# Cosine attention followed by mixture-of-depths: five reorderings around norms, scatters and the last batch

## The chip, the cores and the metric

The kernel runs on one core of a Trainium2 chip. The metric is the device time of one execution in microseconds. A core has five engines with queues of their own, which work in the order of their queues and wait for one another on semaphores: TensorE (PE in the profile; its weight loads are PEld), VectorE (DVE), ScalarE (ACT), GpSimd (POOL) and SyncE (SP, which here only issues transfers).

## The reference

Two parts, one after the other, on 8 batches of 448 tokens.

```python
q_n = q / (np.linalg.norm(q, axis=-1, keepdims=True) + 1e-06)      # 8 x 12 heads x 448 x 64
k_n = k / (np.linalg.norm(k, axis=-1, keepdims=True) + 1e-06)
scores = np.matmul(q_n, k_n.transpose(0, 1, 3, 2)) / tau           # tau = 0.1
attn = softmax(scores);  x = np.matmul(attn, v)                    # heads side by side: 8 x 448 x 768
scores = np.einsum('bsd,d->bs', x, w_gate)
for b in range(B):
    top_idx = np.argpartition(-scores[b], capacity)[:capacity]     # 128 of 448 tokens
    ye = np.maximum(x[b, top_idx] @ w1, 0.0) @ w2                  # 768 -> 1024 -> 768
    g = 1.0 / (1.0 + np.exp(-scores[b, top_idx]))
    out[b, top_idx] = x[b, top_idx] + g[:, None] * ye              # all other tokens: out = x
```

## The kernel before

**Slots.** The 12 heads of a batch are taken as 6 pairs, so there are 48 pairs. The main loop has one slot for each pair. All that is issued in a slot is written out in program order by hand; nothing reorders it later. In slot i the kernel computes the scores of pair i in four pieces c = 0, 3, 1, 2 (`scores`, L273 and L278) and their exponentials (`exps`, L286 and L289); multiplies the exponentials of pair i-1 with v (`pv_tails`, `pv`, L302 and L313); divides and writes pair i-1 of x (`pv_evac`, L329 and L331); transposes q and k of pair i+1 (`transposes`, L255, and its copy out of PSUM, `qkT_copy`, L261); and scales q and k of pair i+2 by their norms on GpSimd (`scale`, L228), which also casts v (`values`, L235) and the finished part of x (`half_x`, L352).

**Norms.** A pair's squares are made on ScalarE (`square`, L185) in the slot that the table `SQ` names, mostly five slots ahead. A slot later TensorE adds them up in groups of eight (`sum_pe`, L192) and VectorE finishes the sum (`sum_dve`, L200). The pairs of a group in the list `NORMS` then share three small steps: `norm_a` on ScalarE (Ln, then Exp of half, for the square root; L208 and L209), `norm_b` on GpSimd (adds 1e-6; L215) and `norm_c` on VectorE (reciprocal; L218). A group of two is done every second slot. `norm_b` stands at the end of the slot, behind `scale`, `values` and `half_x` on GpSimd; `norm_c` stands in the next slot, ahead of gate, x and the copy of the transposed tiles on VectorE. The list `due` carries a group from one to the other; where the first pair of a group is scaled in the same slot, `norm_b` and `norm_c` follow `norm_a` directly.

**Mixture of depths.** When a batch of x is done, its second part is spread over the slots after it. `work` holds functions by slot and place; the places are run in this order within a slot: P1, D0, D1, P1b, A, P2, C, D3, B. The dictionaries `late`, `mid`, `early` and `last` give the slots for each batch, counted from s = 6(b+1), the first slot after the batch.

- `gate` (L359): a product with w_gate and its sum, one column of 128 tokens at a time, on VectorE.
- `rank_prep` (L370 to L373): splits the gates in fp32 into three bf16 terms, on GpSimd.
- `rank_rep` (L391, L395, L398): TensorE spreads the terms over all partitions; with the copy `own` back to one column for each partition.
- `rank_count` (L404): for each token the number of larger gates. `pick` (L412): the 0/1 selection matrix `sel` of 128 by 128, in bf16. Both on VectorE; the last two counts and the four selections stand at place D3 of the batch's rank slot (12, 18, 24, 30, 36, 41 and 46 for batches 0 to 6).
- `select` and `select_b` (L421 to L438): row numbers and gates of the selected tokens.
- `gather` (L461), `ffn1` (L479), `ffn2` (L488): products with the selection, with w1 and with w2; the results leave PSUM by `evac` on VectorE (L443 to L447) or ScalarE (L449).
- `scatter` (L503): an indirect transfer issued by GpSimd that adds the result to the rows of the output. It runs at place P2, behind `half_x` of that slot, in the slot of the last `ffn2`.
- `store_x` (L344, L345): SyncE writes a batch of x to the output. Transfers to the output wait for the ones before it, so a store waits for an earlier scatter to land, and a scatter for the stores.

**The last batch** can't hide behind later slots. The first 640 of its 768 columns are stored early and their part of the gates is summed early (`gc`). The last 128 columns come as `x_last` behind the main loop: they are stored into a copy of the batch in memory (`x_copy`, from which the rows are gathered again as `xs`, L697) and into the output, the gates are completed and counted, and batch 6's two feed-forward layers run beside this. At the end stand the scatter of batch 6 (L503), the gather of `xs` (L697), the sum of `xs` and the result (L709) and the last scatter (L712), all scatters and the gather in GpSimd's queue.

**Loads.** q, k and v come from SyncE in groups of three pairs into a ring of four buffers. A load waits until the group that had its buffer is scaled and cast.

Of the kernel before, what the change touches and what calls it, by code (L numbers as in the profile page):

```python
# [8 lines left out]
FP32 = mybir.dt.float32  # L9
# [8 lines left out]
def kernel(  # L18
# [60 lines left out]
    starts = {g0: gi for gi, (g0, gn) in enumerate(GROUPS)}  # L79
    place = {g0 + g: (gi, g) for gi, (g0, gn) in enumerate(GROUPS) for g in range(gn)}  # L80

    NORMS = [(0, 1), (1, 2)]
    while sum(NORMS[-1]) < N:
        NORMS.append((sum(NORMS[-1]), min(2, N - sum(NORMS[-1]))))
    nplace = {g0 + g: (n, g) for n, (g0, gn) in enumerate(NORMS) for g in range(gn)}
# [76 lines left out]
    w1_sb = const.tile([P, KD, F], BF16)  # L162
    w2_sb = const.tile([P, KF, D], BF16)

    for j in range(NS):
        nc.gpsimd.affine_select(
            out=tie[:, j, :], in_=tie[:, j, :], compare_op=ALU.is_ge,
            fill=-(2.0 ** -126), base=-j * P if j < NC else T - SM, pattern=[[1, S]],
            channel_multiplier=-1)
# [44 lines left out]
    def norm_b(n):  # L214
        nc.gpsimd.tensor_scalar_add(norm_of(n), norm_of(n), 1e-6)  # L215
# [146 lines left out]
            op0=ALU.mult, op1=ALU.add, accum_out=dst[:, j:j + 1])  # L362


    def rank_prep(b, eng=None):
        g = gates[b % 2]
        eng = eng or nc.gpsimd
        sg = moe.tile([P, NS, 3], BF16, name="sg")
        r1 = moe.tile([P, NS], FP32, name="r1")
        eng.tensor_copy(sg[:, :, 0], g)  # L370
        eng.tensor_sub(r1, g, sg[:, :, 0])
        eng.tensor_copy(sg[:, :, 1], r1)
        eng.tensor_sub(sg[:, :, 2], r1, sg[:, :, 1])  # L373
        st[b]["sg"] = sg
# [10 lines left out]
    def rank_rep(b):  # L385
        sg = st[b]["sg"]
        rep = bank()
        for j in range(NS):
            c0, n = (j * P, P) if j < NC else (SM, T)
            for e in range(3):  # L390
                nc.tensor.matmul(out=rep[:, c0:c0 + n],  # L391
                                 lhsT=sg[:, j, e:e + 1].to_broadcast([P, P]),
                                 rhs=iden_b[:, P - n:], start=(e == 0), stop=(e == 2))
        for e in range(3):
            nc.tensor.matmul(out=rep[:, S:S + NS], lhsT=iden_b, rhs=sg[:, :, e],  # L395
                             start=(e == 0), stop=(e == 2))
        own = moe.tile([P, NS], FP32, name="own")
        nc.vector.tensor_copy(own, rep[:, S:S + NS])  # L398
        st[b].update(rep=rep, own=own)

    def rank_count(b, j):
        r = slice(0, P) if j < NC else slice(T, P)
# [108 lines left out]
    def at(slot, where, fn, *args):  # L511
        work.setdefault((slot, where), []).append((fn, args))

    def run(slot, where):
        for fn, args in work.pop((slot, where), []):
# [2 lines left out]

    late = dict(gate=((2, "D1"), (3, "D1"), (4, "D1"), (5, "D1")), rep=5, rank=6, select=7,
                ffn=((8, "B"), (9, "B"), (10, "B"), (11, "A")))  # L520
    mid = dict(late, ffn=((8, "B"), (9, "A"), (9, "B"), (10, "A")))
    early = dict(gate=((2, "D1"), (3, "D1"), (3, "D1"), (4, "D1")), rep=4, rank=5,
                 select=6, ffn=((7, "B"), (8, "A"), (8, "B"), (9, "A")))
    last = dict(gate=((1, "D1"), (2, "D1"), (2, "D1"), (3, "D1")), rep=3, rank=4,
                select=5, ffn=())
    for b in range(B - 1):
# [15 lines left out]
        if b < B - 2:  # L542
            at(s + m["select"] + 1, "A", gather, b, 1)
        for (d, w), (fn, n) in zip(m["ffn"], ((ffn1, 0), (ffn1, 1), (ffn2, 0), (ffn2, 1))):
            at(s + d, w, fn, b, n)
            if fn is ffn2 and n == 1:
                at(s + d, "P2", scatter, b)
    bb = B - 1
    gc = const.tile([P, NS], FP32)

# [7 lines left out]

    SQ = {}
    for p in range(3, N):  # L560
        SQ.setdefault({3: 0, 4: 0, 5: 1, 6: 2}.get(p, p - 5), []).append(p)
    SW = 2 * NB7 * D8

    wps = bank()
# [11 lines left out]
    for ps in ((0,), (1, 2)):  # L576
        sc = ps_sc.tile([P, 2, 512], FP32, name="sc")
        for p in ps:
            square(p)
        sums(ps, sc)  # L580
        for m, p in enumerate(ps):
            sum_dve(p, sc[:, 1, m * SW:(m + 1) * SW])
        norm_a(nplace[ps[0]][0])
        norm_b(nplace[ps[0]][0])
        norm_c(nplace[ps[0]][0])
        if ps[0] == 0:
            warm(24)
            scale(0, True)
            transposes(0)
            qkT_copy(0)  # L590
        else:
            scale(1)
    values(0)
    values(1)

# [1 line left out]
    for i in range(N + 1):  # L597
# [10 lines left out]
        if prev:  # L608
            pv_tails(i - 1)
        exps(i, 0)  # L610
        for p in SQ.get(i, []):
            square(p)
        run(i, "D0")
        sc = ps_sc.tile([P, 2, 512], FP32, name="sc")
# [25 lines left out]
            qkT_copy(i + 1)  # L640
        scores(i, 2)
        exps(i, 2)
        if i < 2:
            transposes(i + 1)
            qkT_copy(i + 1)
        if i + 2 < N:
            scale(i + 2)
            values(i + 2)
        if prev:
            half_x(i - 1)  # L650
        due = [n for n in due if NORMS[n][0] != i + 2]
        for n in due:
            norm_b(n)
        run(i, "P2")
        run(i, "C")
        run(i, "D3")
# [10 lines left out]
    pv(N - 1)  # L667
    pv_evac(N - 1)
    gather(b, 1, "A", True)
    store_x(bb, x_last, 5 * P, D, x_copy)  # L670
    store_x(bb, x_last, 5 * P, D)
    g7 = gates[bb % 2]
    xg = moe.tile([P, P], FP32, name="xg", bufs=1)
    nc.gpsimd.tensor_mul(xg, x_last[:, NC], wg_b[:, 5 * P:D])
    for j in range(NC):
        gate(bb, j, 5 * P, D, gc, g7, x_last)
    xgs = moe.tile([P, P], FP32, name="xgs", bufs=1)
    gd = moe.tile([P, 1], FP32, name="gd", bufs=1)
    nc.scalar.activation(xgs, xg, AF.Copy, accum_out=gd)
    nc.vector.tensor_add(g7[:, NC:], gd, gc[:, NC:])  # L680
    ffn1(b, 0, "A", True)
    rank_prep(bb, nc.vector)
    nc.scalar.activation(xh_last, x_last, AF.Copy)
    ffn1(b, 1, "A", True, 0, lambda: rank_rep(bb))
    ffn2(b, 0, "A", True)
    ffn2(b, 1, "A", True)
    for j in range(NS):
# [62 lines left out]
```

## Time and profile before

Three runs gave 280.02 us (median), from 279.03 to 280.46. The profiled execution has a span of 281.0 us.

| engine | busy us | share of the span | instructions |
|---|---|---|---|
| TensorE | 234.4 | 83% | 4591 |
| TensorE's weight loads | 176.0 | 63% | 4591 |
| VectorE | 178.5 | 64% | 477 |
| ScalarE | 203.3 | 72% | 318 |
| GpSimd | 166.9 | 59% | 228 |

The busy share is an average over slots with different limits. Slots in which ScalarE sets the pace last about 4.05 us; slots with feed-forward or selection work last 4.5 to 6 us; slot 33 lasted 8.5 us. A row of the profile's waits names the waiting instruction, the one that ended the wait, the sum of the waits in us, how often, and the longest. A timeline row has the start, the duration, the engine, the line and the operands of an instruction, or of several alike (x4); in brackets stands the idle time before it and what ended that.

### The profile page before, as it was taken

The page shows a single profiled execution, that of the slowest core. Times are in us where ns is not written, and L with a number is a line of the kernel's source. Part 1 is how long each engine was busy: PE and PEld are TensorE (multiplying, and loading weights), DVE is VectorE, ACT ScalarE, POOL GpSimd, SP SyncE. Part 2 cuts the span into 40 slices and gives each one's busy share as a digit, 9 for nine tenths or more (in the row PEclk, how much of TensorE's full clock was granted, in tenths as well). Part 3 has the DMA queues.
Part 4 walks back from the last instruction along what each step waited for, and adds up shares of the span by engine and source line. Part 5 has one row for each costly group of instructions (what it writes and reads, how often), then busy time and mean ns, then how long its engine had stood idle before and what let it go on. Part 6 is the DMA issues. An engine that isn't in the chain of part 4 may idle for free. (4 is left out here: it accounts for less than half of the span.)

```text
span 281.0 us, 10601 instructions
## 1 busy us (share of the span) xinstructions
PE 234.4 (83%) x4591; PEld 176.0 (63%) x4591; DVE 178.5 (64%) x477; ACT 203.3 (72%) x318; POOL 166.9 (59%) x228
## 2 busy tenths in 40 slices
PE   7498787688899979988979979699899798979970
PEld 6377565456677757756657757476685576657750
DVE  1333544456877786758864786467877778788611
ACT  3779999967988778869775778578776884665410
POOL 5447578849666677459471777357755864651231
PEclk9979999959999999999997999799999999986995
DMA  7999999999999849994799449992760164046851
GB/s 256 283 278 288 301 296 303 301 236 282 272 303 248 213 65 210 277 265 75 178 264 272 104 58 206 274 264 51 119 138 3 11 135 113 3 59 155 240 93 77
DMA packets 32431, 53.18 MB, mean 189 GB/s; under 512 B 2176, under 2 KB 28672, under 8 KB 31488
## 3 DMA queue, kind: packets, MB, share of 16 engines
q1 hardware_dynamic: 28976, 45.13, 60.0%
q0 software_dynamic: 2992, 6.69, 14.0%
q8 instruction: 36, 0.59, 0.9%
q10 hardware_dynamic: 416, 0.69, 0.7%
q14 instruction: 11, 0.09, 0.1%
HBM read 40.11 MB, written 15.53 MB: 198 GB/s over the span
## 5 line engine op out<-in xcount | busy, mean ns | idle before, releaser
L286 ACT ACTIVATE expS<-sc 128x896 bf16<-128x896 f32 x144 | 126.0, 916 | 27.7 <-PE sc L273 27.3
L228 POOL TENSOR_TENSOR qkn<-qk_raw,rs 128x896 bf16<-128x896 f32 (+1 forms) x48 | 82.0, 1708 | 68.1 <-PE qkT_ps L255 46.6
L273 PE MATMUL sc<-qkT 64*128 64x448 bf16 x288 | 54.2, 372 | 19.0 <-DVE qkT L261 10.1
L313 PE MATMUL o_ps<-vo,expS 128*128 128x65 bf16 x1152 | 46.5, 197 | 3.0 <-issue 3.0
L185 ACT ACTIVATE sq<-qk_raw 128x896 bf16<-128x896 f32 x48 | 45.1, 945 | 2.3 <-DMA qk_raw<-in_k_dram 2.3
L313 PEld LDWEIGHTS <-expS 128*128 128x128 bf16 x1152 | 42.3, 100 | 3.5 <-issue 3.1
L273 PEld LDWEIGHTS <-qkT 64*128 64x128 bf16 x288 | 15.3, 93 | 42.5 <-issue 21.8
L289 ACT ACTIVATE expS<-sc 128x448 bf16<-128x448 f32 x48 | 25.7, 536 | 21.3 <-PE sc L278 21.1
L261 DVE COPY qkT<-qkT_ps 128x960 bf16<-128x960 bf16 x48 | 31.4, 654 | 14.2 <-PE qkT_ps L255 9.9
L331 DVE TENSOR_TENSOR x_b<-o_ps,rden 128x512 f32<-128x512 f32 x47 | 32.5, 691 | 1.6
L255 PEld LDWEIGHTS <-qkn 64*64 64x64 bf16 x1344 | 25.6, 111 | 12.5 <-issue 8.9
L255 PE MATMUL qkT_ps<-iden_b,qkn 64*64 64x64 bf16 x1344 | 31.0, 196 | 2.5 <-POOL qkn L228 1.6
L352 POOL CAST xh<-x_b 128x512 bf16<-128x512 f32 x47 | 30.8, 656 | 2.9 <-DVE gr L424 2.9
L359 DVE CUSTOM_DVE_ANT_0 junk<-x_b,wg_b 128x768 bf16<-128x768 f32 (+1 forms) x32 | 30.0, 937 | 0.2
L192 PE MATMUL sc<-sq,iden_b 128*128 128x112 bf16 x384 | 28.0, 220 | 1.9 <-ACT expS L286 1.6
L200 DVE TENSOR_REDUCE ss<-sc 128x14 f32<-128x112 f32 x48 | 12.8, 273 | 25.9 <-PE sc L192 25.6
L235 POOL CAST vo<-v_raw 128x448 bf16<-128x448 f32 x48 | 27.4, 572 | 0.0
L479 PEld LDWEIGHTS <-w_sb 128*128 128x128 bf16 x384 | 23.2, 101 | 6.5 <-issue 5.8
L192 PEld LDWEIGHTS <-iden_b 128*128 128x128 bf16 x384 | 21.7, 101 | 4.3 <-issue 1.4
L479 PE MATMUL m_ps<-xeT,w_sb 128*128 128x128 bf16 x288 | 19.4, 226 | 3.8 <-issue 2.2
L404 DVE SCALAR_TENSOR_TENSOR junk<-m_ps,own,tie 128x448 bf16<-128x448 f32 (+1 forms) x32 | 21.7, 679 | 0.7
L488 PE MATMUL m_ps<-w_sb,hT 128*128 128x384 bf16 x96 | 17.6, 326 | 0.9 <-DVE hT L443 0.9
(88 smaller groups left out, 265.3 us busy)
## 6 DMA issues: line engine op xcount, KB each, us to landing
qk_raw<-in_q_dram SPq DMA_DIRECT2D x15, 672.0 KB, 9.2
qk_raw<-in_k_dram SPq DMA_DIRECT2D x15, 672.0 KB, 11.2
v_raw<-in_v_dram SPq DMA_DIRECT2D x30, 192.0 KB, 10.0
out_dram<-x_b SPq DMA_DIRECT2D x7, 768.0 KB, 7.8
v_raw<-in_v_dram SPq DMA_DIRECT2D x30, 144.0 KB, 8.7
out_dram<-x_b SPq DMA_DIRECT2D x7, 576.0 KB, 4.7
w_sb<-in_moe_w_dram POOLq DMA_DIRECT2D x2, 1536.0 KB, 19.2
out_dram<-x_b SPq DMA_DIRECT2D x1, 640.0 KB, 6.5
```

Of the source, the lines that this page charges most:

```text
L185: nc.scalar.activation(sq_tiles[p], raw[gi % NRAW][0][:, :, g].rearrange("p a b d -> p a (b d)"), AF.Square)
L192: nc.tensor.matmul(out=dst, lhsT=iden_b, rhs=sq[:, :, s * D8:(s + 1) * D8], start=(s == 0), stop=(s == Dh // D8 - 1))
L228: eng.tensor_mul(kn[:, :, b0:b1], qk[:, :, g, b0:b1], rs[:, m, :, b0:b1].rearrange("p a (b o) -> p a b o", o=1) .to_broadcast([P, 2, b1 - ...
L255: nc.tensor.transpose(out=qkT_ps[r, o:o + T], in_=kn[r, a, s], identity=iden_b[r, r], tile_position=(u * T, u * T))
L261: nc.vector.tensor_copy(qkT_tiles[p], qkT_ps[:, :W])
L273: nc.tensor.matmul(out=sc[:, u, :S], lhsT=qkT[r, KO + c * P:KO + (c + 1) * P], rhs=qkT[r, :S], start=True, stop=True, tile_position=(u * D ...
L286: nc.scalar.activation(ex[:, 2 * c:2 * c + 2], sc[:, :, :S], AF.Exp, scale=inv_tau)
L313: nc.tensor.matmul(out=o_ps[:, u, j * E:(j + 1) * E], lhsT=ex[:, 2 * c + u, qc(j)], rhs=vo[:, u * NS + c], start=False, stop=(c == NC - 1) ...
L331: nc.vector.tensor_mul(dst.rearrange("p j (u d) -> p j u d", u=2), o[:, :, :, :Dh], rden.to_broadcast([P, NS, 2, Dh]))
L352: nc.gpsimd.tensor_copy(xh_tiles[b][:, :, c], x_tiles[b][:, :, c])
L359: nc.vector.tensor_tensor_reduce(out=junk[:, d0:d1], in0=src, in1=wg_b[:, d0:d1], scale=1.0, scalar=0.0 if prev is None else prev[:, j:j + 1],
L479: nc.tensor.matmul(out=ps[:, f * CAP:(f + 1) * CAP], lhsT=w1_sb[:, t, fc * P:(fc + 1) * P], rhs=xeT[t], start=(m == 0) if cut else (t == 0 ...
```

## The change

There are five groups of edits.

1. **Scatters a slot later.** Each scatter of batches 0 to 5 moves to place P2 of the slot after its last `ffn2`.
2. **The norms' small term ahead of the scaling.** `norm_b` moves ahead of `scale`, `values` and `half_x` in GpSimd's queue.
3. **The head of the kernel.** Pairs 3 and 4 get norm groups of their own; the square of pair 3 is the last of ScalarE's work in slot 0, and that of pair 4 moves to slot 1; pair 1 is scaled half by GpSimd and half by VectorE, as pair 0 was.
4. **Two evacuations on ScalarE.** In slots 39 and 44 the second half of `ffn1` leaves PSUM on ScalarE in place of VectorE (place "AA" of `mid` and `early`).
5. **The last batch.** The gates are spread in fp32 by one matmul for each column with an fp32 identity, ahead of and without the three-term split and the copy `own`; the split still feeds `select`, and moves to GpSimd. The output's x_last store stands ahead of that of `x_copy`. Batch 6's first `ffn1` takes its first four k tiles first. ScalarE's part of the last gate column stands ahead of VectorE's columns.

```diff
-    NORMS = [(0, 1), (1, 2)]
+    NORMS = [(0, 1), (1, 2), (3, 1), (4, 1)]
...
+    iden_f = const.tile([P, P], FP32)
+    nc.gpsimd.tensor_copy(iden_f, iden_b)
...
+    def rank_rep_last(b):
+        g = gates[b % 2]
+        rep = bank()
+        for j in range(NS):
+            c0, n = (j * P, P) if j < NC else (SM, T)
+            nc.tensor.matmul(out=rep[:, c0:c0 + n],
+                             lhsT=g[:, j:j + 1].to_broadcast([P, P]),
+                             rhs=iden_f[:, P - n:], start=True, stop=True)
+        st[b].update(rep=rep, own=g)
...
-    mid = dict(late, ffn=((8, "B"), (9, "A"), (9, "B"), (10, "A")))
+    mid = dict(late, ffn=((8, "B"), (9, "AA"), (9, "B"), (10, "A")))
...
-                 select=6, ffn=((7, "B"), (8, "A"), (8, "B"), (9, "A")))
+                 select=6, ffn=((7, "B"), (8, "AA"), (8, "B"), (9, "A")))
...
-            at(s + d, w, fn, b, n)
+            at(s + d, w[0], fn, b, n, "A" if w == "AA" else "D")
             if fn is ffn2 and n == 1:
-                at(s + d, "P2", scatter, b)
+                at(s + d + 1, "P2", scatter, b)
...
-        SQ.setdefault({3: 0, 4: 0, 5: 1, 6: 2}.get(p, p - 5), []).append(p)
+        SQ.setdefault({3: 0, 4: 1, 5: 1, 6: 2}.get(p, p - 5), []).append(p)
...
-            scale(1)
+            scale(1, True)
...
-        for p in SQ.get(i, []):
+        for p in SQ.get(i, []) if i else []:
             square(p)
...
         exps(i, 2)
+        if i == 0:
+            square(3)
         if i < 2:
             transposes(i + 1)
             qkT_copy(i + 1)
+        due = [n for n in due if NORMS[n][0] != i + 2]
+        for n in due:
+            norm_b(n)
         if i + 2 < N:
             scale(i + 2)
             values(i + 2)
         if prev:
             half_x(i - 1)
-        due = [n for n in due if NORMS[n][0] != i + 2]
-        for n in due:
-            norm_b(n)
...
     gather(b, 1, "A", True)
+    store_x(bb, x_last, 5 * P, D)
     store_x(bb, x_last, 5 * P, D, x_copy)
-    store_x(bb, x_last, 5 * P, D)
...
-    for j in range(NC):
-        gate(bb, j, 5 * P, D, gc, g7, x_last)
     xgs = moe.tile([P, P], FP32, name="xgs", bufs=1)
     gd = moe.tile([P, 1], FP32, name="gd", bufs=1)
     nc.scalar.activation(xgs, xg, AF.Copy, accum_out=gd)
+    for j in range(NC):
+        gate(bb, j, 5 * P, D, gc, g7, x_last)
     nc.vector.tensor_add(g7[:, NC:], gd, gc[:, NC:])
-    ffn1(b, 0, "A", True)
-    rank_prep(bb, nc.vector)
+    ffn1(b, 0, "A", True, 4)
+    rank_prep(bb)
     nc.scalar.activation(xh_last, x_last, AF.Copy)
-    ffn1(b, 1, "A", True, 0, lambda: rank_rep(bb))
+    ffn1(b, 1, "A", True, 0, lambda: rank_rep_last(bb))
```

More of the change, by code (lines that the diff above doesn't have):

```diff
@@ L362, in gate, with rank_prep @@
             op0=ALU.mult, op1=ALU.add, accum_out=dst[:, j:j + 1])
-    def rank_prep(b, eng=None):
+    def rank_prep(b, eng=nc.gpsimd):
         g = gates[b % 2]
-        eng = eng or nc.gpsimd
         sg = moe.tile([P, NS, 3], BF16, name="sg")
```

## The prediction

> **What bounds the kernel now.** I read the page first, then the windows of single slots, the waits, and the timeline round each wait. No engine bounds the whole run:
>
> ```profile
> PE 234.4 (83%) x4591; PEld 176.0 (63%) x4591; DVE 178.5 (64%) x477; ACT 203.3 (72%) x318; POOL 166.9 (59%) x228
> ```
>
> So the limit has to be found slot by slot. A slot runs from the first exponential of a head pair to that of the next (slot 0 starts at 11.25, slot 47 at 250.54). The windows of slots 8, 9, 18 and 19: length, then busy us of TensorE, its weight loads, VectorE, ScalarE and GpSimd, clock, DMA:
>
> ```profile
> 47.74:51.79 4.05, 3.21 (x77) 2.49 (x76) 2.54 (x6) 4.02 (x8) 3.70 (x6) 1.00 0.97 330
> 51.79:57.93 6.14, 3.30 (x75) 2.31 (x74) 2.80 (x7) 3.86 (x6) 5.54 (x7) 0.86 1.10 276
> ...
> 97.21:101.33 4.12, 3.08 (x77) 2.25 (x75) 3.33 (x9) 4.09 (x7) 3.94 (x5) 1.00 0.33 44
> 101.33:107.05 5.72, 5.03 (x106) 3.68 (x101) 4.58 (x16) 4.21 (x9) 3.88 (x5) 1.00 0.60 113
> ```
>
> and three rows of the waits (sum, times, longest):
>
> ```profile
> DVE rs L218 <- POOL rs L215: 9.9, 12, 1.8
> ...
> PE sc L273 <- DVE qkT L261: 10.1, 11, 2.7
> ...
> PE m_ps L421 <- DVE sel L412: 2.9, 5, 0.7
> ```
>
> Slots 8 and 18 (4.05, 4.12) are full of ScalarE (4.02, 4.09): three wide exponentials, a narrow one, a square, sometimes a norm; that is the floor. Slot 9 (6.14) has no full engine: a chain of waits. Slot 19 has TensorE busy 5.03 of 5.72. Slot 9 in the timeline:
>
> ```profile
> 53.65 0.61 POOL L352 CAST xh<-x_b 128x512 bf16<-128x512 f32 x1
> ...
> 54.35 0.28 POOL L215 TENSOR_SCALAR rs<-rs 128x28 f32<-128x28 f32 x1
> 54.66 0.33 DVE L218 RECIPROCAL rs<-rs 128x28 f32<-128x28 f32 x1 [1.84 <-POOL rs L215]
> ...
> 57.27 0.55 PE L273 MATMUL sc<-qkT 64*128 64x448 bf16 x2 [2.67 <-DVE qkT L261]
> ```
>
> VectorE stops at `norm_c` until GpSimd, behind on scale, cast and half_x, comes to the 0.28 us `norm_b`; gate, x_b and qkT queue behind, and TensorE waits 2.67. Slots 18 and 19:
>
> ```profile
> 98.78 1.71 POOL L503 DMA_INDIRECT out_dram<-oe,idx  x1 [0.18 <-DVE rden L329]
> 98.79 0.69 DVE L331 TENSOR_TENSOR x_b<-o_ps,rden 128x512 f32<-128x512 f32 x1
> ...
> 100.21 0.66 DVE L261 COPY qkT<-qkT_ps 128x960 bf16<-128x960 bf16 x1 [0.73 <-PE sc L273]
> ...
> 102.24 1.58 DVE L412 TENSOR_SCALAR sel<-iota_r,rank 128x128 bf16<-128x128 bf16 x4
> 102.47 0.80 POOL L352 CAST xh<-x_b 128x512 bf16<-128x512 f32 x1
> ...
> 103.39 0.67 PE L421 MATMUL m_ps<-tokc,sel 128*128 128x2 bf16 x4 [0.65 <-DVE sel L412]
> ```
>
> The transposes end at 99.52, yet the qkT copy starts at 100.21: 1.44 us after the scatter started. In slots 24, 30, 36 and 46 the gap from scatter to copy is 1.45, 1.43, 1.43, 1.38. So I read the copy as held by the scatter, not by the matmul named. The copy delays the two rank counts and the selections behind it, and TensorE waits 0.65. The tail:
>
> ```profile
> 264.53 0.61 SPq L345 DMA_DIRECT2D out_dram<-x_last  x1
> ...
> 268.27 1.60 POOL L503 DMA_INDIRECT out_dram<-oe,idx  x1 [3.65 <-ACT gr L437]
> 269.31 2.76 PE L488 MATMUL w_ps<-w_sb,hT 128*128 128x384 bf16 x16
> 270.18 1.02 POOL L697 DMA_INDIRECT xs<-x_copy,row  x1 [0.30 <-issue]
> 275.27 1.14 DVE L709 SCALAR_TENSOR_TENSOR oe<-w_ps,gr,xs 128x384 f32<-128x384 f32 x2 [4.94 <-DMA xs<-x_copy,row]
> ```
>
> The output's x_last store lands at 267.31 (chain), releases the scatter of batch 6, behind which GpSimd gathers xs; TensorE was done at 272.07, 3.2 before xs.
>
> [...] The trace agrees for the selections: four take 0.74 at 251.39 with GpSimd quiet, 1.58 beside its casts. [...] I measure the scatter from its start to the copy's.
>
> **The change part by part.**
>
> *norm_b ahead of scale.* It runs while GpSimd waits for transposes anyway (46.6 us at L228, 29 times), so the 0.28 costs nothing. `norm_b` is a new wait ahead of scale, values and half_x: it waits for ScalarE's Exp, and behind it the transposes of the next slot wait for scale. ScalarE's Exp is done before scale may start (slot 30: 162.70, transposes 162.89), and scale ends 0.5 (slot 8) to 4 us before those transposes. Hidden. VectorE's wait vanishes outside the first slots. Slot 9: the reciprocal moves from 54.66 to 52.85, where the squares' sum before it on VectorE ends; then gate (0.9), rden (0.2), x_b (0.69, ends 55.0), copy (0.65, ends 55.65), scores at 55.7 against 57.27. The transposes that the copy needs end at 54.3, so they don't hold it; ScalarE's last exponential ends 55.65, so it doesn't absorb it: 1.6. Slot 11 (wait 0.92): sg then waits for the weight load's issue, which gains only the 0.28 and a gap: 0.4. Slot 41 (0.96): ScalarE's floor leaves 0.5 of 4.65. Slot 43 (0.56): 0.4. Slots 5 and 7 (3.81, 3.91) sit on the floor: 0. Sum 2.9.
>
> *Scatters a slot later.* Slots 18, 24, 30, 36 lose the 0.7 hold of the copy. They are on ScalarE's floor themselves; the gain comes in 19, 25, 31, 37, where sel was awaited 0.65, 0.56, 0.53, 0.52. Now the scatter follows half_x of the same slot, just when the selections are due. The selections wait from about 101.6, half_x ends about 102.5, and a scatter has started 0.16 to 0.18 after its predecessor: [...] Then 4 x 0.55 = 2.2. If the scatter takes it first, selections start at 102.7 + 1.43 = 104.1 instead of about 103.1: a loss of 1.0, in five slots (42 too). I take the gain and keep both. For 42 and the gain in 43 together I count half: of 0.3 and 0.4, 0.35. Stores of whole batches wait for the scatter's landing (store 104.76, scatter 98.78 + 5.7) and hold SyncE's loads about 4 us longer; a load issued at 106 feeds squares at about 132: hidden.
>
> *Head.* Slot 0 gets rid of two squares (2 x 0.95) ahead of its exponentials, and the split shortens scale(1) from 1.69 to 1.33: slots 1 and 2 start 1.0 and 1.2 earlier. But slot 2 was full of ScalarE (4.51 of 4.51), gets one more Ln/Exp pair (0.22 + 0.23), and VectorE now waits in it for norm_a(4), norm_b, norm_c before x_b and qkT: scores(3,0) at about 26.9 less at most 0.4. Left: 0.3.
>
> *First feed-forward halves on ScalarE (slots 39, 44).* hT was awaited 0.66 and 0.24; exponential c3 moves back 0.43. Slot 39 gains 0.4, slot 44 nothing.
>
> *Last batch.* fp32 spreading takes 15 matmuls (1.08 + 0.22), four conversions (0.8) and the own copy off; four fp32 matmuls come. No row here shows an fp32 matmul. Bounds: 0.25 us in all if they cost what the bf16 ones do (twelve in 0.76, 63 ns each), 2.0 if eight times that, an estimate[...]. Either way it feeds the branch with 3.2 us of slack: 0. The k tiles 0 to 3 first in ffn1 spare TensorE its 0.25 us for xeT at 258.63, on the same branch; the conversions on GpSimd (0.2 each) and the accumulation on ScalarE ahead of the gates lie beside the gates and counts: 0. iden_f lies in GpSimd's idle start, 0. The output's x_last store now goes before x_copy's, worth some 1.4 (half of the 3.1 us in which these rows were written). But batch 5's scatter moves from 247.99 to after half_x(45), 249.4; the 640-column store waited for its landing (253.73) and moves 1.4 too, and the write stream that follows is full. Sum of the tail: 0.
>
> Sum: 2.9 - 0.4 (slot 43, in the half) + 2.2 + 0.35 + 0.3 + 0.4 = 5.75: 280.0 - 5.7 = 274.3.
>
> **The rivals.**
> 1. [...] Time: without the sel gains (2.55) and with 5 x 1.0 lost: 274.3 + 2.55 + 5.0 = 281.9, slower.
> 2. *Gains are absorbed.* For: ScalarE's floor of 4.05, and TensorE's pauses put down to issue (2.2 at 147, 2.4 at 178) and clock drops can fall elsewhere. Against: slot 9 has 2.2 us over the floor. Slot 9 and half the rest: 280.0 - 1.6 - 0.3 = 278 to 279.5.
> 3. *The tail gains.* If batch 5's scatter didn't hold the store, 1.4 more: 272.9. Against: store and landing meet at 253.7.
>
> **How the numbers follow.** Forecast and its upside 0.62, absorbed 0.22[...]. Of the absorbed case four tenths is still faster than 278.6: faster 0.62 + 0.09 = 0.71, same 0.13, slower 0.16. The range goes from the tail's 272.9 less 1.4 for a profile whose pauses fall well, to 280.5[...].
>
> **What would show it.** L218's wait on L215 should fall from 9.9 to about 4, all before 35 us; slot 9 to about 4.5; the copies in slots 18, 24, 30, 36 should start with the end of the transposes; the wait of L421 for sel vanish; the scatter start after the selections. The xs gather should still follow the scatter of batch 6 at once. I am wrong if sel starts 1.4 us after a scatter, or if slots 19, 25, 31, 37 grow.

## The result and the profile after

The changed kernel takes 269.34 us, the median of four runs from 266.48 to 273.03; beside it the kernel before took 279.52 (278.89 to 280.46). The ratio is 0.960, with a 95% interval from 0.951 to 0.969. In two later measurements it was 0.963 (0.957 to 0.968) and 0.956 (0.950 to 0.961). The forecast was 274.3 with a range from 271.5: the direction was right, 10.2 us were gained where 5.7 were forecast, and the time lies below the range. The profiled executions took 282.8 and 268.4 us, so the two traces differ by 14.4 where the medians differ by 10.2, and a size that is read from this pair alone is too large for a usual execution.

First what the forecast had named. Busy times of the changed kernel, from its page, and three rows of its waits (sum, times, longest):

```profile
PE 225.2 (84%) x4584; PEld 169.9 (64%) x4584; DVE 175.2 (66%) x472; ACT 203.3 (76%) x322; POOL 168.3 (63%) x234
```

```profile
PE sc L275 <- DVE qkT L263: 7.3, 13, 1.2
DVE rs L220 <- POOL rs L217: 7.2, 5, 2.4
...
PE m_ps L433 <- DVE sel L424: 1.0, 4, 0.4
```

The wait of VectorE for `norm_b` (L220 on L217, formerly L218 on L215) has gone from twelve times to five. All five lie before 30 us, where pairs 3 and 4 now have groups of their own; their sum is 7.2, where the forecast had about 4. TensorE's wait for the selections fell from 2.9 to 1.0.

The windows of slots 8, 9, 18 and 19 of the changed kernel (length, then busy us of TensorE, its weight loads, VectorE, ScalarE and GpSimd, clock, DMA share, GB/s):

```profile
47.51:53.20 5.69, 3.26 (x81) 2.35 (x80) 2.62 (x6) 4.38 (x8) 5.16 (x7) 1.00 1.01 375
53.20:57.10 3.90, 3.14 (x82) 2.27 (x77) 2.72 (x7) 3.81 (x6) 2.53 (x4) 1.00 1.09 284
95.21:99.69 4.48, 3.25 (x77) 2.29 (x76) 3.49 (x10) 4.14 (x8) 2.75 (x5) 1.00 0.59 131
99.69:105.00 5.31, 4.80 (x102) 3.56 (x101) 4.18 (x16) 4.21 (x8) 4.91 (x5) 1.00 0.28 29
```

Slot 9 fell from 6.14 to 3.90 and slot 19 from 5.72 to 5.31. But slots 8 and 18 grew by 1.6 and 0.4, and in each TensorE stands for a time put down to issue: 1.5 and 0.8.

Slots 18 and 19 in the timeline of the changed kernel (start, duration, engine, line, operands, idle time before and what ended it):

```profile
97.84 0.63 PE L257 MATMUL qkT_ps<-iden_b,qkn 64*64 64x64 bf16 x28
...
98.51 0.66 DVE L263 COPY qkT<-qkT_ps 128x960 bf16<-128x960 bf16 x1
...
100.53 1.24 DVE L424 TENSOR_SCALAR sel<-iota_r,rank 128x128 bf16<-128x128 bf16 x4
100.75 0.62 POOL L354 CAST xh<-x_b 128x512 bf16<-128x512 f32 x1
...
101.48 0.53 PE L433 MATMUL m_ps<-tokc,sel 128*128 128x2 bf16 x3 [0.30 <-DVE sel L424]
101.55 1.71 POOL L515 DMA_INDIRECT out_dram<-oe,idx  x1 [0.18 <-issue]
```

The transposes end at 98.47 and the copy starts 0.04 later; it had come 0.7 after them. The selections start a microsecond ahead of the scatter, so the first rival, in which the scatter goes first and five slots lose 1.0 each, didn't come about.

Now slots 27 and 33, first in the windows of the kernel before, then of the changed one:

```profile
142.71:150.39 7.68, 5.47 (x105) 4.23 (x99) 3.74 (x9) 3.80 (x5) 3.65 (x6) 0.87 1.03 278
175.35:183.81 8.46, 6.09 (x106) 4.55 (x101) 3.73 (x9) 4.08 (x6) 3.65 (x6) 0.80 0.86 244
```

```profile
138.53:143.04 4.51, 4.51 (x106) 3.60 (x101) 3.45 (x9) 3.80 (x5) 2.57 (x4) 1.00 0.95 217
168.08:172.60 4.52, 4.52 (x106) 3.61 (x101) 3.46 (x9) 3.81 (x6) 2.58 (x4) 1.00 0.95 219
```

The same work took 7.1 us less in these two slots, more than all the parts that the forecast had priced. No scatter and no selection lies in them. In the changed kernel TensorE is busy from end to end; before, it stood 2.2 and 2.4 us for nothing that the profile names, and the clock granted afterwards was lower: 0.50 from 148.40 to 151.81 and from 179.12 to 182.53.

The tail, from slot 46 to the end, took 34.6 before and takes 34.8 now:

```profile
243.23 1.36 PE L408 MATMUL m_ps<-iden_f,gate 128*128 128x128 f32 x8 [0.55 <-DVE gate L361]
...
253.78 1.60 POOL L515 DMA_INDIRECT out_dram<-oe,idx  x1 [6.30 <-DMA x_copy<-x_last]
256.14 1.02 POOL L711 DMA_INDIRECT xs<-x_copy,row  x1 [0.76 <-issue]
```

As before, the scatter of batch 6 waits for the stores of x_last and the gather of xs follows it. The four fp32 matmuls (L408; each appears as two instructions) take 1.36 us, between the forecast's bounds of 0.25 and 2.0.

### The profile page after: what moved, and what is told of

Read it like the earlier page. It is cut to its first block, busy times and chain, and to the rows that moved or that the text cites. A ratio compares the mean times of both kernels' runs of the same rounds, so it can differ in the third digit from the quotient of the medians.

```text
span 266.6 us, 10588 instructions
## 1 busy us (share of the span) xinstructions
PE 225.2 (84%) x4584; PEld 169.9 (64%) x4584; DVE 175.2 (66%) x472; ACT 203.3 (76%) x322; POOL 168.3 (63%) x234
## 4 chain that ended last, share of the span: by engine, by line
PE 35%; DMA 21%; DVE 16%; ACT 12%; issue 7%; SPq 4%; POOL 3%; POOLq 1%; ACTq 0%
DMA v_raw<-in_v_dram 11%; PE m_ps L491 7%; ACT expS L288 7%; PE m_ps L500 6%; PE sc L275 6%; PE o_ps L315 5%; DVE junk L416 4%; DVE junk L361 3%; DMA qk_raw<-in_k_dram 3%; DMA qk_raw<-in_q_dram 3%; PE sc L194 3%; ACT expS L291 3%; PE qkT_ps L257 3%; DVE xeT L457 2%; DVE x_b L333 2%
## 5 line engine op out<-in xcount | busy, mean ns | idle before, releaser
L288 ACT ACTIVATE expS<-sc 128x896 bf16<-128x896 f32 x144 | 125.3, 917 | 17.0 <-PE sc L275 16.4
L230 POOL TENSOR_TENSOR qkn<-qk_raw,rs 128x896 bf16<-128x896 f32 (+1 forms) x48 | 80.3, 1673 | 36.4 <-PE qkT_ps L257 26.3
L275 PE MATMUL sc<-qkT 64*128 64x448 bf16 x288 | 52.3, 358 | 14.8 <-DVE qkT L263 7.3
L315 PE MATMUL o_ps<-vo,expS 128*128 128x65 bf16 x1152 | 44.6, 193 | 1.5 <-issue 1.5
L315 PEld LDWEIGHTS <-expS 128*128 128x128 bf16 x1152 | 40.3, 97 | 2.1 <-issue 1.7
L354 POOL CAST xh<-x_b 128x512 bf16<-128x512 f32 x47 | 29.7, 633 | 2.0 <-DVE gr L436 1.3
L194 PE MATMUL sc<-sq,iden_b 128*128 128x112 bf16 x384 | 26.9, 215 | 2.4 <-ACT expS L288 2.3
L217 POOL TENSOR_SCALAR rs<-rs 128x28 f32<-128x28 f32 (+1 forms) x26 | 8.0, 307 | 25.8 <-ACT rs L211 21.7
L491 PEld LDWEIGHTS <-w_sb 128*128 128x128 bf16 x384 | 22.2, 98 | 3.3 <-issue 3.1
L416 DVE SCALAR_TENSOR_TENSOR junk<-m_ps,own,tie 128x448 bf16<-128x448 f32 (+1 forms) x28 | 19.0, 678 | 0.5
L491 PE MATMUL m_ps<-xeT,w_sb 128*128 128x128 bf16 x288 | 18.1, 219 | 1.3 <-DVE xeT L457 1.3
```

Of the source, the lines that this page charges most:

```text
L194: nc.tensor.matmul(out=dst, lhsT=iden_b, rhs=sq[:, :, s * D8:(s + 1) * D8], start=(s == 0), stop=(s == Dh // D8 - 1))
L230: eng.tensor_mul(kn[:, :, b0:b1], qk[:, :, g, b0:b1], rs[:, m, :, b0:b1].rearrange("p a (b o) -> p a b o", o=1) .to_broadcast([P, 2, b1 - ...
L275: nc.tensor.matmul(out=sc[:, u, :S], lhsT=qkT[r, KO + c * P:KO + (c + 1) * P], rhs=qkT[r, :S], start=True, stop=True, tile_position=(u * D ...
L288: nc.scalar.activation(ex[:, 2 * c:2 * c + 2], sc[:, :, :S], AF.Exp, scale=inv_tau)
L315: nc.tensor.matmul(out=o_ps[:, u, j * E:(j + 1) * E], lhsT=ex[:, 2 * c + u, qc(j)], rhs=vo[:, u * NS + c], start=False, stop=(c == NC - 1) ...
L491: nc.tensor.matmul(out=ps[:, f * CAP:(f + 1) * CAP], lhsT=w1_sb[:, t, fc * P:(fc + 1) * P], rhs=xeT[t], start=(m == 0) if cut else (t == 0 ...
```

## The experiments

The profiles are compared by stages, read from the starts of the slots' first exponentials. Times in us; "to 12" is the start of slot 12, "17 to 46" runs from the start of slot 17 to that of slot 46, "rest" from there to the end.

```
kernel                              to 12   17 to 46   rest   slots 27+33   slots 19+25+31+37
before (first profile, again)    69.0, 70.3  154.4, 151.4  34.6, 34.6  16.1, 13.4   22.6, 22.1
head alone; tail alone           69.2, 68.7  154.8, 153.6  34.2, 34.2  15.4, 16.2   21.9, 22.7
norm alone; norm and head        69.2, 72.2  150.2, 150.1  34.7, 34.5  14.5, 12.5   22.9, 23.1
before, 64 idle matmuls          69.1        148.3         35.8        10.1         22.0
burst alone moved (twice)        70.7, 69.7  147.6, 146.1  35.2, 35.4   9.0,  9.0   23.9, 22.0
scatters alone (twice)           68.9, 70.3  143.3, 143.4  35.5, 35.4   9.0,  9.0   19.6, 19.8
changed, norm_b put back         71.5        143.0         34.4         9.0         20.1
changed (three profiles)   66.8, 70.7, 67.4  141.7, 140.0, 141.2  34.8, 34.5, 35.0  9.0, 9.0, 9.0  20.5, 19.9, 20.5
changed, 64 idle matmuls         68.4        141.8         34.9         9.0         20.4
```

**Each part alone.** Four kernels, each the kernel before with one group of the edits.

```diff
-                at(s + d, "P2", scatter, b)
+                at(s + d + 1, "P2", scatter, b)
```

> The kernel before with one edit: every scatter of a batch's result is issued one slot later. Theory A (the forecast's sizes hold part by part, and the 4.5 us that were missed come from elsewhere): 2.2 for slots 19, 25, 31, 37 and 0.35 for slots 42 and 43, less up to 1.4 in the tail, where batch 5's scatter now holds the last big output store: 277 to 278. Theory B (the scatter's part was sized too small, since a held copy also moves pauses and clock drops): 272 to 274. Theory C (the parts gain only together): within 0.5 of the kernel before.

Measured: 0.968 (0.957 to 0.980) of the kernel before. Slots 19, 25, 31 and 37 fell together from 22.6 to 19.6, but the slots behind them (20, 26, 32, 38) grew from 20.2 to 21.8; slot 42 fell by 0.8. Slots 27 and 33 fell to 9.0. The time is that of theory B, but the part that was too small is not the hold of the copy: it is one that the forecast had not counted, the 7.1 us in slots 27 and 33.

```diff
+        due = [n for n in due if NORMS[n][0] != i + 2]
+        for n in due:
+            norm_b(n)
         if i + 2 < N:
             scale(i + 2)
...
         if prev:
             half_x(i - 1)
-        due = [n for n in due if NORMS[n][0] != i + 2]
-        for n in due:
-            norm_b(n)
```

> The kernel before with one edit: the norms' small GpSimd term (norm_b) goes ahead of scale, values and half_x. Theory A: slot 9 falls from 6.1 to about 4.5, slots 11, 41 and 43 by about 0.4 each: 277.1. Theory B (norm_b is the part that was sized too small): 272 to 274. Theory C: within 0.5 of the kernel before.

Measured: 1.000 (0.994 to 1.006). Slot 9 did fall, from 6.14 to 4.74, and slots 41 and 43 by 0.5 and 0.7. But slot 12 starts at 69.2, where it started at 69.0 before: slot 6 held a TensorE pause of 1.9, and its window shows the transfers full.

```profile
39.86:46.62 6.76, 4.48 (x77) 2.82 (x76) 1.83 (x4) 4.32 (x8) 3.52 (x5) 0.75 1.10 275
54.41:59.15 4.74, 3.18 (x76) 2.25 (x76) 3.42 (x7) 3.92 (x6) 4.66 (x5) 1.00 1.10 285
```

These are slots 6 and 9 of the kernel with norm_b alone. Both have the DMA engines busy throughout (1.10 of their count, 275 and 285 GB/s). In every kernel 18.4 to 19.7 MB are moved before slot 12, in 66 to 72 us, with the DMA share at 1.0 on average. Nor is the length of slot 9 a sign of norm_b: it lies between 4.5 and 6.1 in the ten profiles without norm_b ahead, and between 3.9 and 5.5 in the ten with it. That the loads set the time there is read from these shares; no run changed the loads.

The head (the edits of `NORMS`, `SQ`, `square(3)` and `scale(1, True)`) and the tail (all edits of group 5) alone:

> The kernel before with the head's edits alone: norms of pairs 3 and 4 apart, the first slot's square last and one of its two squares moved to slot 1, scale of pair 1 split between two engines. Theory A: 0.3 faster, 279.7. Theory B (the head is what was sized too small): 276 to 278; the start of slot 8 then comes 2 or more earlier than in the kernel before. Theory C: within 0.5 of the kernel before.

> The kernel before with the tail's edits alone: the last batch's gates spread in fp32, the output's x_last store ahead of the one to x_copy, the first feed-forward matmul's order, the small conversions on GpSimd. Batch 5's scatter stays where it was, so the forecast's cancelling doesn't take place. Theory A: 0 to 1.4 faster, 278.6 to 280. Theory B (the tail was sized too small): 275 to 277, with a tail from the start of slot 47 of 26 to 28 in place of 30.5. Theory D (fp32 spreading and the new order cost time): 281.

Measured: 0.985 (0.972 to 0.998) and 0.989 (0.977 to 1.001). In the trace the head's edits bring slot 6 forward by 0.3, as forecast, and nothing is left of it at slot 12 (69.2). The tail's edits alone shorten the rest by 0.4. Slot 8 doesn't start 2 earlier, as theory B of the head would have it, but 0.3. The interval of the head's ratio lies below 1 and would allow more than the trace shows; as the kernel before, timed as if it were a new one, came out at 0.995 (0.990 to 1.001), what the head gives in time stays open.

**What the pauses are.** The profile's page names a queue that moves no data of the kernel:

```profile
q8 instruction: 36, 0.59, 1.0%
```

36 packets with 0.59 MB, so 16.4 KB each; TensorE runs 4584 matmuls and as many weight loads, which is 36 times 255. So these look like its instructions, in blocks of 256, 128 of them weight loads. Counting weight loads in the traces bears it out: from 12 to 245 us the 20 profiles hold 58 pauses of TensorE of 0.5 us or more that are put down to issue, and every one begins after a weight load whose number is 96 more than a multiple of 128 (2528 and 3040 in slots 27 and 33 of the kernel before). And in all 58, TensorE goes on 0.9 to 1.8 us after a packet of that queue has ended; among the 653 times that it enters a block in this stretch, it never does so earlier than 0.9 us after the end of the packet that brings it. So I read the pauses as TensorE waiting for its next block of instructions. The blocks ahead of these two pauses last 5.6 and 6.0 us, and the packet of the next one comes while a block runs: in the kernel before it starts between 1.1 us ahead of TensorE's entry into the block and 5.7 behind it. This is how late the fetch's packet starts after TensorE enters a block, by the packets of that queue in the trace (the changed kernel and those moved alone: one profile each):

```
kernel                     block 18   block 20   block 22   pauses after them
before (two profiles)      5.7, 5.1   1.8, 2.0   5.6, 5.2   2.2, 1.8 (slot 27)   -     2.4, 2.1 (slot 33)
burst alone moved            0.2        5.3        0.3          -          1.3 (slot 30)    -
scatters alone              -0.2        5.2        2.5          -          1.4 (slot 30)    -
changed                     -0.3        5.1        1.4          -          1.1 (slot 30)    -
```

With a DMA share of 0.03 to 0.06 a fetch starts from 0.5 us ahead of TensorE's entry to 0.1 behind it (blocks 29 and 32 of the kernel before, 28 and 32 of the changed one). In the blocks of the table it starts 5.1 to 5.7 late where TensorE enters the block after SyncE has begun to put a batch's store and the loads behind it in the queues, as in blocks 18 and 22 before: in the kernel before that burst begins at 135.2 and block 18 at 139.9; in the changed kernel the block begins at 135.6, just ahead of the store at 135.8. A store waits for the landing of an earlier scatter (SyncE stood at it six times for that in the kernel before, 101.6 us in all; the store of 135.2 follows the scatter of 129.5 by 5.8), so a scatter that comes a slot later moves the burst by about 5 us against TensorE's stream. Two kernels test this from both sides, one moving TensorE's stream and leaving the burst, one moving the burst and leaving the scatters.

```diff
-        if i < 3:
+        if i < 11:
             warm(8)
         run(i, "B")
```

> The kernel before with 64 idle matmuls more, 8 at the end of each of slots 3 to 10, where TensorE has slack. Nothing else is changed: from slot 11 on, TensorE's instruction stream is the same, moved by half a fetched block of 256 instructions. Theory F (the pauses of 2.2 in slot 27 and 2.4 in slot 33 are TensorE waiting for its next block of instructions, which comes in the middle of the burst of a batch's store and loads): the fetches now come half a block earlier, before the burst; slots 27 and 33 fall from 7.7 and 8.5 to about 4.5 each, and the kernel takes 273 to 277. Any pause that remains starts at another instruction than in the kernel before. Theory G (the pauses belong to those two slots' own work, or to the scatter): slots 27 and 33 stay at 7 to 8.5, 280 to 281.

> The changed kernel with the same 64 idle matmuls. Theory F: the block that was fetched at 135.3, just ahead of the store at 135.8, now falls at about 139, in the burst; one or both pauses of about 2 come up in slots 25 to 33, and the kernel takes 272 to 276. Theory G: 269 to 270, with slots 27 and 33 at 4.5.

Measured: 0.994 (0.989 to 0.999) for the kernel before with the shift, 0.981 (0.974 to 0.988) for the changed one, beside 0.971 (0.965 to 0.977) for a close relative of it (below) on the same chip. In the first, the pauses of 27 and 33 at their old instructions are gone and slot 27 is at 4.5. But the time of 273 to 277 wasn't reached: three other blocks now came late, with pauses of 0.9 in slot 33 and of 1.0 and 1.3 in slots 21 and 35. In the second a pause of 1.4 came up in slot 24, not in 25 to 33, and the kernel came out 1% longer than that relative, with intervals that overlap. So half a block of shift moves the pauses, as theory F has it; what it takes away in one place it puts back in another.

```diff
-        at(s, "P2", store_x, b)
+        held = b >= 2
+        if held:
+            at(s + 2, "P2", hold, b + 1)
+        at(s + 2 * held, "P2", store_x, b)
+        if held:
+            at(s + 2, "P2", loads, s)
```

`hold` is the copy of 512 bytes, `loads` are the loads that stood in slot s + 1 and are taken out there.

> The kernel before with its scatters where they were, so that the copies of slots 18, 24, 30 and 36 stay held and the selections late. Only the burst is moved: from batch 2 on, SyncE's stores of a batch, and the loads behind them, wait for the x of the next batch's second head pair (a copy of 512 bytes in SyncE's queue, which waits for it), about where they come in the kernel with the scatters a slot later. Theory F (most of the late scatters' gain is that the burst of stores and loads no longer meets TensorE's fetch of instructions): slots 27 and 33 fall to about 4.5 each, slots 19, 25, 31 and 37 stay at 5.6 to 5.7, and the kernel takes 273 to 277, ratio 0.97 to 0.985. Theory S (the gain is in the copy's hold, and the pauses go with it): slots 27 and 33 stay at 6.5 to 8.5, and the ratio is 0.995 or more.

Measured: 0.997 (0.992 to 1.002). The slots are as theory F has them, 27 and 33 at 4.5 each and 19 and 25 at 5.6 and 5.5, but the time isn't, and the expected 0.97 to 0.985 was missed: the first 92 us were 4 longer in this profile, and a pause of 1.5 with a clock drop lengthened slots 30 and 31 by 2.8. Two of the other three kernels on that chip were as late there, so the three kernels in question ran once more together:

> The kernel before, once more. Theory F: slots 27 and 33 at 5.8 to 8.5 with a TensorE pause for no visible cause in each, at the same two instructions as in the other kernels with early scatters. If the pauses are an accident of the first profile: both slots at about 4.5.

> The burst of stores and loads moved alone, once more. From the start of slot 17 to that of slot 46: 145 to 148 by the first trace, against 150 to 155 in the kernels with early scatters. Theory F: 2 to 5 us below the kernel before. If the burst alone gives nothing: within 1 us, and the pauses come back in other slots.

> The late scatters alone, once more. Theory F: from slot 17 to 46 about 143; below the moved burst by the copy's hold, 2.6 by the slots (four times 0.85 and 0.67, less 1.5 in the slots behind them). If the late scatter has a gain of its own beyond hold and burst: 5 or more below the moved burst with the same pauses.

Measured: 0.995 (0.990 to 1.001) for the kernel before, 0.987 (0.976 to 0.997) for the burst alone and 0.987 (0.978 to 0.997) for the scatters alone. The kernel before has both pauses again, at the same two instructions. TensorE round slot 27 in its timeline and slots 27 and 33 in its windows:

```profile
147.39 0.34 PE L479 MATMUL m_ps<-xeT,w_sb 128*128 128x128 bf16 x3
149.55 0.66 PE L479 MATMUL m_ps<-xeT,w_sb 128*128 128x128 bf16 x9 [1.81 <-issue]
```

```profile
144.79:151.42 6.63, 4.82 (x105) 3.70 (x99) 3.69 (x9) 3.80 (x6) 3.65 (x6) 0.96 1.02 292
176.83:183.59 6.76, 4.68 (x106) 3.67 (x101) 3.73 (x9) 3.92 (x6) 2.96 (x5) 1.00 0.98 280
```

and with the burst alone moved, where the three matmuls before the pause and the 21 behind it run as one:

```profile
145.31 1.51 PE L479 MATMUL m_ps<-xeT,w_sb 128*128 128x128 bf16 x24
```

```profile
142.70:147.22 4.52, 4.52 (x106) 3.61 (x101) 3.55 (x9) 3.81 (x6) 2.96 (x5) 1.00 1.10 245
172.68:177.20 4.52, 4.52 (x106) 3.61 (x101) 3.55 (x9) 3.81 (x6) 2.96 (x5) 1.00 1.08 241
```

From slot 17 to 46 the traces of this chip give 151.4, 146.1 and 143.4: 5.3 for the burst, 2.7 more for the rest of the late scatters. The times show less than half of the first (0.995 to 0.987 is about 2.3, with intervals that overlap) and nothing of the second. So the moved burst takes the pauses away in both of its profiles, but how much of the kernel's time they cost is not settled by these times. In size the late scatters stay between 0.968 and 0.987, whose intervals just overlap.

The second profile of the kernel before also answers a reading of the forecast, that the scatter holds the copy in its slot. Slots 18 and 19 in it:

```profile
101.18 1.71 POOL L503 DMA_INDIRECT out_dram<-oe,idx  x1 [0.18 <-DVE junk L404]
101.45 0.63 PE L255 MATMUL qkT_ps<-iden_b,qkn 64*64 64x64 bf16 x28
...
102.12 0.66 DVE L261 COPY qkT<-qkT_ps 128x960 bf16<-128x960 bf16 x1
...
104.15 1.91 DVE L412 TENSOR_SCALAR sel<-iota_r,rank 128x128 bf16<-128x128 bf16 x4
```

The scatter again starts ahead of the transposes, but the copy starts 0.04 after their end. It is not held in slots 18, 24, 30 and 36 of five profiles with early scatters (this one, norm and head, 64 idle matmuls, and both of the burst alone); in the other four (the first one of the kernel before, and head, tail and norm alone) it is held by 0.6 to 0.7. Slots 19, 25, 31 and 37 are about as long either way, 22.1 against 22.6 in the two profiles of the kernel before. What sets their length is the end of the selections: in 76 of 80 cases the slot ends 3.2 after it. In the kernel before the four selections took 1.5 to 1.6 where the copy was held and 1.9 to 2.0 where it wasn't; with late scatters they take 1.2 to 1.3. So the early scatter delays the selections in two forms, of which the held copy is one. What decides between the forms isn't shown.

**norm_b once more.** The changed kernel with norm_b put back behind `half_x`, and the kernel before with norm_b ahead and the head's edits:

> The changed kernel with norm_b put back behind half_x, all else as changed. The forecast's price: slots 9, 11, 41 and 43 lose 2.9, so 272.2. Theory H (slot 9's gain is absorbed by the loads that the first 69 us wait for, as the kernel with norm_b alone suggests; only slots 41 and 43, and the slots behind a scatter, lose): 270 to 271.5.

> The kernel before with norm_b ahead of scale and the head's edits, the scatters and the tail as they were. The forecast's prices: 2.9 + 0.3, ratio 0.9886. Theory H (up to slot 12 the loads set the time, so the two together gain there 0 to 2, and 1.1 in slots 41 and 43; the pauses of slots 27 and 33 stay): slot 12 starts at 67 to 69, slots 27 and 33 at 6.5 to 8.5, ratio 0.988 to 0.997.

Measured: 0.974 (0.966 to 0.982), beside 0.971 for the relative of the changed kernel; and 0.996 (0.991 to 1.002). With norm_b put back the slots are nearer to theory H than to the forecast's price, but the time can't decide between 270 to 271.5 and 272.2. With norm and head the forecast's ratio of 0.9886 lies outside the interval and theory H's range holds, but two of its other numbers were missed: slot 12 started at 72.2 instead of 67 to 69, and slot 27 took 5.8 instead of 6.5 or more. Slots 17 to 46 lose 1.3 to 3.0 without norm_b ahead: slot 41 is 4.6 instead of 3.7, slot 43 5.8 instead of 5.2, and slots 20, 26, 32 and 38 together 21.3 instead of 20.5. The start of slot 12 lies anywhere from 66.8 to 70.7 in the changed kernel itself and at 72.2 with norm and head alone: nothing of slot 9's gain can be told there.

**A version that beats both.** Batch 5's scatter goes back to slot 45 of the program (GpSimd comes to it during slot 46 of the trace) while those of batches 0 to 4 stay late, and then also four fifths of the early store to `x_copy` go to slot 46.

```diff
-                at(s + d + 1, "P2", scatter, b)
+                at(s + d + (b < B - 3), "P2", scatter, b)
...
-    at(N - 1, "P2", store_x, bb, None, 0, 5 * P, x_copy)
+    at(N - 2, "P2", store_x, bb, None, 0, 4 * P, x_copy)
+    at(N - 1, "P2", store_x, bb, None, 4 * P, 5 * P, x_copy)
```

> The changed kernel with batch 5's scatter alone back at slot 45; the six others stay a slot later. If the tail's loss (31.7 from the start of slot 47 against 30.1 with the tail's edits alone) is the last big store waiting for that scatter's landing: the tail falls to about 30.2, slot 46 grows from 3.2 to 4.1, and the kernel is 0.4 to 0.8 faster than the changed one. If the end is set by the write stream all the same: no difference or up to 0.9 slower.

> The changed kernel with batch 5's scatter back at slot 45, again, now beside the changed kernel on the same chip. In its first profile slot 46 and the tail took 33.85 together, against 34.84 in the changed kernel: 0 to 1 faster than the changed kernel.

> The changed kernel again, beside the others on the same chip: ratio 0.955 to 0.97.

> The changed kernel with batch 5's scatter at slot 45, and four fifths of the last batch's store to x_copy issued in slot 46, where the queues are nearly idle, instead of in the full write stream at the end. The 512 of 640 columns took about 3.5 of that stream's time; the output's x_last store and the scatter behind it should move up by 2 to 3.5, until TensorE's branch ends last. Expected 2 to 3 faster than the changed kernel: ratio 0.945 to 0.955. If the end hangs on the gates' branch all the same: no difference.

> The version with batch 5's scatter at slot 45 and the early store to x_copy, beside the changed kernel: the rest from slot 46 in 32.5 to 33, so 1.5 to 2.5 faster than the changed kernel. If the first version's time was an accident of its chip: within 0.5.

> The changed kernel beside the improved version on one chip: ratio to the kernel before 0.955 to 0.970; slots 17 to 46 in 140 to 142, the rest from slot 46 in 34.5 to 34.9.

The scatter alone: 0.971 (0.965 to 0.977) and 0.952 (0.945 to 0.958), the latter beside 0.963 (0.957 to 0.968) for the changed kernel on the same chip: about 1% if anything. Its rest is 33.8 and 33.7 against 34.5 to 35.0, though slot 46 didn't grow as expected: its 4.1 belonged to the first profile of the kernel before, where its copy was held, and in the second one it takes 3.2 with the same scatter. With the early store: 0.955 (0.945 to 0.965), and again 0.941 (0.936 to 0.947; 264.8 us) beside 0.956 (0.950 to 0.961; 269.0 us) for the changed kernel on the same chip. These intervals don't meet: it is the fastest of all. Its tail in the timeline:

```profile
231.91 0.61 SPq L347 DMA_DIRECT2D x_copy<-x_b  x1
...
249.64 1.60 POOL L516 DMA_INDIRECT out_dram<-oe,idx  x1 [4.18 <-DMA x_copy<-x_last]
```

The large store to x_copy is issued at 231.91, when the queues are nearly empty (a DMA share of 0.01 in the 2.1 us before), and batch 6's scatter starts 19.9 after the start of slot 46 (229.78) instead of 22.0.

## Why the prediction was right in direction and short by 4.5

- **norm_b ahead of scale: 2.9 forecast.** The mechanism was right in that VectorE's late waits are gone. The place was wrong: slots 9 and 11 (2.0 of the 2.9) lie where the DMA engines are full, and their gain can't be told at slot 12, nor by slot 9 itself, which scatters by 1.6 from profile to profile without the edit. The forecast had the DMA share of slot 9 (1.10) on its page and asked only for the next engine. Slots 41 and 43 gave 1.6 instead of 0.9, and 0.8 came up behind the scatters, where nothing was forecast.
- **The copy's hold: 2.2 + 0.35 forecast.** The size was right, the reading only in part. Slots 19, 25, 31 and 37 fell by 2.3 between burst alone and scatters alone, and slot 42 by 0.7 to 1.0; but in the profile of the burst alone no copy of these slots was held, and what shrank was the time of the selections. The slots behind them give back 1.1 to 1.5, which norm_b ahead takes down to 0.2. The reason isn't shown: four selections took 1.58 at 102.24 of the kernel before, with casts of GpSimd beside them, and 0.74 at 251.39, where GpSimd had no instruction; for the copy five profiles speak against a hold by the scatter.
- **The scatter goes ahead of the selections: the first rival, didn't come.** In slots 19, 25, 31, 37 and 42 of the changed kernel the selections start 1.0 to 1.1 ahead of it.
- **Head 0.3, ScalarE's half 0.4.** Right in the trace: 0.3 at slot 6, absorbed later; slot 39 fell from 6.3 (scatters alone) to 6.0 and slot 44 by 0.1.
- **Tail 0.** Right: 34.6 before, 34.5 to 35.0 after. The two sides that were to cancel: the tail's edits alone give 0.4, and batch 5's scatter put back in the changed kernel takes 0.7 to 1.3 off. (The 0.8 to 0.9 more of the scatters alone is no measure of it: the burst alone, with this scatter early, has 0.6 to 0.8 more as well.)
- **Gains are absorbed: the second rival.** Its sum doesn't follow from its words: slot 9 and half of the rest of 5.7 would give 276.3, where it takes off 0.3 for the half.
- **The step that failed** is the sentence that "TensorE's pauses put down to issue (2.2 at 147, 2.4 at 178) and clock drops can fall elsewhere", with no price in the sum. They don't fall just anywhere: in all six profiles with early scatters and an unmoved burst they are there, at the same two instructions, and cost 3.5 to 7.1 in slots 27 and 33 (5.4 in the kernel with norm_b alone, whose execution took 279.1). I read them as TensorE's wait for a block of instructions, whose packet started 5.1 to 5.7 late in the burst of a batch's store and loads; they go when the burst is moved. With it failed "Stores of whole batches wait for the scatter's landing ... hidden". The forecast saw that the late scatters move the burst, by 4 us in its reckoning, and asked only which load would then be late. It didn't ask what else is moved beside those loads: the 36 packets of q8.

Put together, the terms that were priced come to about the forecast 5.7 (2.4 for norm_b, 3 for the scatters, 0.5 for ScalarE's half), and the pauses are what was missing: 1.4 in slots 22 and 23, 4.4 to 7.1 in 27 and 33, less about 0.7 for a new one in slot 30. These are sizes from traces; they add up to 11 to 14, more than the 10.2 measured, and what takes the rest back isn't shown. That the pauses go with the burst is shown by the moved burst; their part of the time is shown in direction by one of its two measurements (0.987, whose interval lies below 1; the other, 0.997, doesn't exclude 1), and in size not at all.

## What to carry to other kernels

Idle time of an engine that nothing explains is not noise until a second profile of the same kernel shows it elsewhere: count that engine's instructions up to it, and look for a fixed step, as the 128 weight loads here. A hold that one profile shows needs the second profile as well: here it was gone, and the slot behind was as long. Where the page shows a queue of instructions beside those of the data (q8 here), ask of every moved transfer which of its packets it will now meet, not only who consumes it. And before pricing a chain of waits, read the DMA share of its slot: at the 1.10 of slot 9 no gain could be told.

## What the runs showed of the hardware

- The queue `q8 instruction` moved 36 packets of 16.4 KB, and the 58 pauses of TensorE lie on a step of 128 weight loads, with as many matmuls 256 instructions. In a burst of stores and loads a packet started up to 5.7 us after TensorE had entered the block before (139.87 and 145.57 in the kernel before), and TensorE never went on earlier than 0.9 us after its end (1.4 and 1.0 at the two pauses there). When the fetch was asked for isn't in the trace.
- Eight of the eleven pauses of 1.8 us or more in slots 12 to 45 come with 3.4 us of half clock, which begin between the moment TensorE resumes and 1.5 us later: at 148.4 after 147.86 and at 179.1 after 178.64 in the kernel before, with a granted clock of 0.50 for 3.41 us each. Its two pauses of 2.2 and 2.4 lengthened slots 27 and 33 by 3.2 and 3.9; one of 2.1 without such a drop lengthened slot 33 by 2.2. Stretches of half clock begin at 56.24, 148.40, 179.12 and 250.80 in the kernel before, which lie 27, 9 and 21 steps of 3.413 us apart. On the grid of their own trace, the eight pauses with a drop have 1.8 us or more inside one step (the two of the kernel before between 144.99 and 148.40 and between 175.71 and 179.12), and the three without are cut by a border into parts of at most 1.7. That the place in the grid decides is read from these eleven pauses alone. In slots 27 and 33 the two together cost 3.5 where neither brought a drop, 4.4 and 5.4 where one did, and 6.4 to 7.1 where both did.
- An fp32 matmul of 128 by 128 by 128 appears as two instructions; the four, the last with half the columns, took 1.36 us together, 0.34 each on average, against 0.063 for each bf16 one that did this spreading in the kernel before.
